# Two of four pairs of attention heads turned by TensorE, twelve weight splits half on GpSimd, and the second matrix's conversions issued behind the Fourier mix

## The chip, the cores and the metric

The kernel runs on one core of a Trainium2 chip. The metric is the device time of one launch, in microseconds; for the kernel before it is 1125.69 us (median of three runs, 1124.08 to 1126.49).

## What is computed

Three blocks follow each other. With four batches of 576 tokens, eight heads of 64, and a model width of 512:

```python
scale = 1.0 / np.sqrt(D)
scores = scale * q @ k.T                       # per batch and head
cum = np.cumsum(np.maximum(s, 0), -1)
bias = -(cum[:, None] - cum[None, :])
scores = np.where(causal, -1e9, scores + np.minimum(bias, 0))
attn = softmax(scores) @ v                     # x: (4, 576, 512)

u = x + np.real(np.fft.fft(np.fft.fft(x, axis=1), axis=2))
y = u + np.maximum(layernorm(u) @ w_ch1, 0) @ w_ch2          # 512 -> 2048 -> 512
out = y + np.maximum((layernorm(y) * g_ln) @ w2_ch1, 0) @ w2_ch2
```

The weight matrices arrive as float64, though the computation is in float32 precision. The kernel takes most products in parts: a number is held as a float16 high half (`hi`) and a float16 rest (`lo`), and three products of halves are summed.

## The kernel before

**Attention.** A batch is worked on in four pairs of heads. A pair's tokens lie in five tiles A0, A1, M, B1, B0, whose causal widths are 129, 257, 320, 448 and 576 keys (`EXT`), that is 2, 3, 3, 4 and 5 key blocks of 128 (`NKB`). A unit is one tile of one head, so a pair has ten units. For a unit, TensorE makes the scores (L1034 and L1039, in fp32 for batches 0 and 1, which are run by `attn_steps32`), VectorE adds the bias and takes the minimum in one reduction (L1040, the name `sc`), and `emit_exp` lets ScalarE take the exponential twice: L777 writes the float16 `hi` into the buffer `p`, L778 writes fp32 in place and accumulates the row sum `rs`. GpSimd clears the columns beyond the width (L776). `emit_lo` subtracts `hi` from the fp32 value to give `lo` (L788, all on GpSimd in batch 0) and then issues DMA transposes on SP's queue, one for each head of B0 and B1 (L792) and one for both heads of each of A0, A1 and M (L800): seven a pair, 14 in two pairs. The transposed halves `pT` are the stationary operand of `emit_pv` (L822, three products a key block), issued five units after the scores, and VectorE normalises the result into `xset` or `xm` (L835).

**Weights of the first MLP.** Class `Weights`: each matrix is cut into 16 pieces of 128x512, pieces 0 to 15 of the first matrix and 16 to 31 of the second, 512 KB each as float64. `load` (L143) fetches a piece on SP's queue into one of nine places of staging (seven tiles of their own and the two halves of `xset_108`). `convert` turns float64 into fp32 by three integer operations on VectorE (L150, L153, L156). `square` (L167) has ScalarE sum the squares. `scale` works out a power of two for a matrix from these sums; the name is `wasc`. `split` makes the halves of a piece: `hi` on ScalarE with the scale (L194), `lo` on VectorE (L195). For pieces named in `POOL1` (none before) or, for the second MLP, `POOLB`, another form is used: ScalarE scales in place (L190) and copies to float16 (L191), and GpSimd subtracts (L192). The generator `prep` runs these as 65 steps: nine loads, 16 conversions of the first matrix, its scale, four splits, six loads, 16 conversions of the second matrix with the other twelve splits between them, and an end. The second matrix is split later, within the MLP.

**What sets the order.** A scheduler orders each engine's instructions by priorities and dependencies; an engine then runs its own list strictly in order. The steps of `prep` are handed out by `more_weights`, which issues them after a score reduction of batch 0's attention: by its end, 42 + `W2PRE` of the 65. The others are given out by `weights_after` in the Fourier mix of batch 0, `QF[n]` after its n-th step. `MARK` = 30 gates batch 1's attention behind the conversion of piece 30.

**Mix and normalisation.** After batch 0's attention, its tokens are folded with a reversed copy (`xo` L1114 on GpSimd, `xe` L1113) and split (`eo`, L1122 and L1123), multiplied along the tokens (`y`, L1141, `yT`, L1145 and L1146) and along the features (`z`, L1182), and added to `x` (`pm` L1197 and L1198, `xset` L1203 to L1205). `emit_ln` takes the statistics (L325 to L363), writes `u` (L348) and turns it by a DMA transpose (`unT`, L349). The first MLP's multiplications begin at L374. They run batch by batch, with the next batch's attention and mix worked in beside them; the second MLP (`wb`) follows.

Of the kernel before, what the change touches and what calls it, by code (L numbers as in the profile page):

```python
# [7 lines left out]
F32 = mybir.dt.float32  # L8
# [3 lines left out]
AF = mybir.ActivationFunctionType  # L12
ALU = mybir.AluOpType
# [6 lines left out]
NPAIR = H // 2  # L20
# [5 lines left out]
A0, A1, M, B1, B0 = range(5)  # L26
EXT = [129, 257, 320, 448, 576]
NKB = [2, 3, 3, 4, 5]
MASKED = -(2.0 ** 120)
KN = {'PVS': (0, 3, 0, 0), 'ORD': ((0, 0, 0), (0, 0, 0), (1, 0, 0), (1, 0, 0)), 'WR4': (1.2, 1.2, 1.2, 1.2), 'W0': 4, 'WRATE': 1.0, 'W2PRE': 18, 'NCONST': 40, 'HOLDN': 1, 'S1': 4, 'S2': 1, 'S1B': 0, 'COST': (1.0, 1.0, 1.0, 1.0, 1.0), 'POOL1': (), 'POOLB': (0, 1, 2, 3, 4, 5, 6, 7), 'QF': (3, 3, 3, 3, 3, 3, 3, 3, 3, 3, 3), 'QL': (1, 1, 1, 1), 'WCALLS': 2, 'WN': 65, 'SPGATE': 0, 'LATE4': 1, 'MARK': 30, 'CJ': (2, 6), 'PVLAG': 7, 'LOLAG': 1, 'PVLAG32': 5, 'PJ32': 4, 'A0OFF': 0, 'A1OFF': 0, 'F0OFF': 300, 'AOFF': (200, 0, 300, 300), 'FOFF': (300, 600, 300, 150), 'LNOFF': (300, 600, 150, 600), 'LOFF': 300, 'PJ': 1, 'PN': 1, 'PL': 6, 'KPREP': 0, 'KPRE': (6, 0, 0), 'KSTEP': ((0, 0, 1), (0, 1), (1,)), 'RATES': (1.9, 1.4, 1.9, 1.2), 'POOLX': (0, 1, 1, 1), 'LO_POOL': ((0, 4, 1, 3, 2), (0, 1, 2, 3), (4,), (0, 1, 2)), 'TAILW': 2, 'LNM': 0, 'LAZY': 8, 'CALLS3': 65, 'N32': 2}  # L30


@with_exitstack
def fused_kernel(ctx: ExitStack, tc, q, k, v, s, wa1, wa2, g_ln, wb1, wb2, tok_c, feat_c, ident_c, rev_c, bias_c, out):
    nc = tc.nc
# [21 lines left out]
    def htile(name, t, h, which):  # L57
        return ring.tile([128, HW[t]], F16, tag=f"h{which}{t}{h}", name=name)

    def htile2(name, t, which):  # L60
        return ring.tile([128, 2 * HW[t]], F16, tag=f"h{which}{t}", name=name)
# [40 lines left out]
    class Weights:  # L102
# [42 lines left out]
        def convert(self, i):  # L145
# [12 lines left out]
            )  # L158
            if i <= KN["MARK"]:
                self.mark = done  # L160
# [52 lines left out]
        def prep(self):  # L213

            for i in range(len(self.wide + self.extra)):
                self.load(i)
                yield KN["COST"][0]
            held = []
            for i in range(16):
# [319 lines left out]
    ident = xpool.tile([128, DM], F32, tag="xm1", name="ident")[:, 0:128]  # L539
# [76 lines left out]
    pairs = {}  # L616
# [127 lines left out]
    def emit_qk(u):  # L744
        P, t, h = pairs[u.p], u.t, u.h
        n = EXT[t]
        cuts = ((0, 288), (288, 576)) if n > 512 else ((0, n),)
        mn = small.tile([128, 2], F32, tag="mn", name="mn", bufs=4)
        kT, qT = P.qkT, q_rows(P, t, h)
        for i, (a, z) in enumerate(cuts):  # L750
            ps = ps_s.tile([128, 512], F32, tag="s", name="s")[:, 0:z - a]
            nc.tensor.matmul(out=ps, lhsT=qT, rhs=kT[:, 2 + h, a:z], start=True, stop=False)
            r = slice(64 * h, 64 * h + 64)
            nc.tensor.matmul(out=ps, lhsT=qT[r], rhs=kT[r, 4, a:z], start=False, stop=True)  # L754
            gate[0] = nc.vector.tensor_tensor_reduce(  # L755
                out=u.f[:, a:z], in0=ps, in1=u.f[:, a:z], scale=P.sc[:, 7:8],
                scalar=mn[:, i - 1:i] if i else 3.0e38, op0=ALU.add, op1=ALU.min, accum_out=mn[:, i:i + 1],
            )
# [95 lines left out]
    N32 = KN["N32"]  # L854

    def attn_steps(b):
# [15 lines left out]
        for i in range(N + KN["PVLAG"]):  # L872
# [23 lines left out]
            if KN["LOLAG"] <= i < N + KN["LOLAG"]:  # L896
                emit_lo(us[i - KN["LOLAG"]])
# [112 lines left out]
    def emit_qk32(u):  # L1010
# [10 lines left out]
        for i, (a, z) in enumerate(cuts):  # L1021
# [16 lines left out]
            if masked:  # L1038
# [283 lines left out]
    if True:  # L1322
# [15 lines left out]
        w = wa.prep()  # L1338
# [152 lines left out]
```

## Time and profile before

| | us |
|---|---|
| runs | 1124.08, 1126.49, 1125.69 |
| median | 1125.69 |
| the profiled execution | 1122.61 |
| its span | 1120.7 |
| TensorE busy | 1005.1 (90%) |
| VectorE busy | 722.8 (64%) |
| ScalarE busy | 569.6 (51%) |
| GpSimd busy | 608.7 (54%) |
| first multiplication of the first MLP (L374) begins | 179.70 |

The profiled execution is one launch seen by the hardware profiler; the span goes from its first to its last instruction. Busy shares are averages over stages with different limits, so the rows further down are taken by stretches of the first 180 us, where the change lies. In the rows PE is TensorE, PEld its weight loads, DVE VectorE, ACT ScalarE, POOL GpSimd and SP the engine that issues most DMAs; L788 is line 788 of the kernel, and `out<-in` are the program's names.

### The profile page before, as it was taken

How to read it: one execution, taken by the hardware profiler on the slowest of the kernel's cores; microseconds unless marked ns; L12 is line 12 of the kernel's file. 1: busy time of each engine (PE TensorE's matmuls, PEld its weight loads, DVE VectorE, ACT ScalarE, POOL GpSimd, SP SyncE). 2: the span in 40 equal slices, each digit the busy share in tenths (PEclk: the TensorE clock that was granted, in tenths of full speed). 3: DMA queues.
4: the chain of work that ended last, by engine and by line, in shares of the span. 5: the costliest groups of instructions: out<-in, count | busy, mean ns of one | idle time of the engine just before them, and what ended most of it. 6: DMA issues, size and time to landing. Idle time of an engine off the chain costs nothing.

```text
span 1120.7 us, 23179 instructions
## 1 busy us (share of the span) xinstructions
PE 1005.1 (90%) x8537; PEld 746.0 (67%) x8537; DVE 722.8 (64%) x1720; ACT 569.6 (51%) x1270; POOL 608.7 (54%) x1298
## 2 busy tenths in 40 slices
PE   5668378988989999889997898998999999999998
PEld 4445245666656566446665675567888888888887
DVE  5978978746798774886746697946544534542333
ACT  5687548764666662566622256643433343443342
POOL 3535658885489640787713106258656546645352
PEclk9878667999999999989999899999999999999999
DMA  7999937666469980289811794102111211211000
GB/s 199 257 201 239 237 106 137 134 132 135 92 123 190 201 183 2 68 163 200 146 36 38 217 310 151 47 1 76 31 46 39 58 20 39 57 39 20 20 8 32
DMA packets 286034, 124.17 MB, mean 111 GB/s; under 512 B 267616, under 2 KB 267872, under 8 KB 285920
## 3 DMA queue, kind: packets, MB, share of 16 engines
q1 hardware_dynamic: 285280, 120.59, 46.6%
q0 software_dynamic: 640, 2.10, 0.6%
q8 instruction: 67, 1.10, 0.4%
q14 instruction: 47, 0.39, 0.1%
HBM read 61.50 MB, written 9.51 MB: 63 GB/s over the span
## 4 chain that ended last, share of the span: by engine, by line
PE 55%; DVE 18%; POOL 7%; DMA 6%; issue 3%; ACT 3%; SPq 1%; POOLq 0%; DVEq 0%; ACTq 0%
PE acc L468 14%; PE g L374 9%; PE g L440 8%; PE g L398 8%; PE g1x L440 8%; DMA pT<-p 3%; PE pv L822 2%; POOL p L788 2%; PE y L1141 1%; PE z L1182 1%; PE s L1034 1%; DVE h L381 1%; PE s L754 1%; POOL sc L732 1%; DVE st L325 1%
## 5 line engine op out<-in xcount | busy, mean ns | idle before, releaser
L374 PE MATMUL g<-unT,wa 128*128 128x256 f16 x1728 | 223.4, 281 | 10.5 <-DMA unT<-u 10.5
L398 PE MATMUL g<-wa,h 128*128 128x512 f16 x864 | 208.1, 383 | 6.6 <-DVE h L381 4.1
L374 PEld LDWEIGHTS <-wa 128*128 128x128 f16 x1728 | 169.4, 101 | 53.7 <-issue 13.2
L454 DVE TENSOR_TENSOR wa<-wa,wa 128x896 f16<-128x896 f32 x72 | 78.9, 1096 | 161.8 <-ACT wa L453 161.7
L468 PE MATMUL acc<-wbbig,wa 128*128 128x256 f16 x1512 | 179.5, 274 | 3.7 <-DVE wa L454 2.4
L440 PEld LDWEIGHTS <-wb 128*128 128x128 f16 x1728 | 169.1, 98 | 20.2
L468 PEld LDWEIGHTS <-wa 128*128 128x128 f16 x1512 | 148.5, 98 | 22.5 <-DVE wa L454 2.8
L398 PEld LDWEIGHTS <-h 128*128 128x128 f16 x864 | 82.4, 99 | 91.4 <-DVE h L381 6.3
L453 ACT CAST wa<-wa 128x896 f16<-128x896 f32 x72 | 67.5, 938 | 142.3 <-POOL wa L451 142.3
L777 ACT ACTIVATE p<-sc,mn 128x576 f16<-128x576 f32 (+4 forms) x160 | 90.5, 578 | 79.3 <-DVE mn L755 26.8
L788 POOL TENSOR_TENSOR p<-sc,p 128x129 f16<-128x129 f32 (+4 forms) x104 | 92.7, 895 | 45.6 <-ACT sc L778 42.2
L450 POOL TENSOR_TENSOR wa<-wa 128x128 f32<-128x128 f32 x72 | 51.8, 720 | 108.1 <-ACT wa L447 108.1
L822 PE MATMUL pv<-v,pT 128*128 128x64 f16 x1632 | 69.9, 199 | 37.1 <-DVE xset L835 12.7
L440 PE MATMUL g1x<-unT,wb 128*128 128x256 f16 x864 | 101.7, 273 | 0.0
L440 PE MATMUL g<-unT,wb 128*128 128x256 f16 x864 | 100.9, 273 | 0.0
L822 PEld LDWEIGHTS <-pT 128*128 128x128 f16 x1632 | 63.3, 102 | 53.3 <-issue 27.2
L778 ACT ACTIVATE sc<-sc,mn 128x576 f32<-128x576 f32 (+4 forms) x160 | 91.9, 575 | 1.8
L732 POOL TENSOR_TENSOR sc<-cumb,ncqs 128x129 f32<-128x129 f32 (+4 forms) x80 | 68.3, 862 | 22.4 <-DVE cumb L642 14.9
L776 POOL MEMSET p<- 128x128 f16 (+1 forms) x160 | 36.7, 249 | 76.0 <-DMA pT<-p 43.7
L1034 PE MATMUL s<-qkT 128*128 128x288 f32 (+4 forms) x192 | 71.4, 468 | 5.5 <-DVE mn L1040 3.0
L381 DVE SCALAR_TENSOR_TENSOR h<-g,h 128x512 f16<-128x512 f32 x72 | 49.1, 682 | 32.6 <-ACT h L380 32.5
L380 ACT ACTIVATE h<-g 128x512 f16<-128x512 f32 x72 | 42.3, 587 | 51.8 <-PE g L374 51.6
(244 smaller groups left out, 1730.7 us busy)
## 6 DMA issues: line engine op xcount, KB each, us to landing
wbbig<-in_moe_w_ch_dram SPq DMA_DIRECT2D x32, 512.0 KB
wa<-in_moe_w_ch_dram SPq DMA_DIRECT2D x21, 512.0 KB
cumb<-cumd SPq DMA_DIRECT2D x24, 288.0 KB
xset<-in_moe_w_ch_dram SPq DMA_DIRECT2D x11, 512.0 KB
x2d<-o SPq DMA_DIRECT2D x18, 256.0 KB
raw<-in_v_dram SPq DMA_DIRECT2D x32, 128.0 KB
out_dram<-wa SPq DMA_DIRECT2D x16, 256.0 KB
raw<-in_k_dram SPq DMA_DIRECT2D x24, 128.0 KB
```

Of the source, the lines that this page charges most:

```text
L374: nc.tensor.matmul(out=ps[:, 256 * i:256 * i + 256], lhsT=ch.w.w1(lw, kk, m + i), rhs=ch.unT[:, 4 * lx + kk, :], start=(n == 0), stop=(n = ...
L398: nc.tensor.matmul(out=ch.ps[j], lhsT=h[:, lh, c:c + 128], rhs=ch.w.w2(lw, m + i), start=(m + i + n == 0), stop=(m + i == MB - 1 and n == 2),)
L440: nc.tensor.matmul(out=ps, lhsT=ch.w.w1(lw, kk, m + 8 * half), rhs=ch.unT[:, 4 * lx + kk, :], start=(n == 0), stop=(n == 11),)
L453: nc.scalar.copy(out=h[:, 0], in_=r[:, 0:7])
L454: nc.vector.tensor_tensor(out=h[:, 1], in0=r[:, 0:7], in1=h[:, 0], op=ALU.subtract)
L468: nc.tensor.matmul(out=acc[key], lhsT=h[:, lh, ia], rhs=b[:, ib, lw], start=(m == 0 and i == 0 and not second), stop=(m == 7 and i == 2 an ...
L732: nc.gpsimd.tensor_tensor(out=u.f[:, 0:n], in0=P.cumb[u.h][:, 0:n], in1=P.ncq[:, t, u.h:u.h + 1].to_broadcast([128, n]), op=ALU.add)
L777: nc.scalar.activation(out=u.w[:, 0:n], in_=u.f[:, 0:n], func=AF.Exp, bias=mn, scale=-1.0)
L778: nc.scalar.activation(out=u.f[:, 0:n], in_=u.f[:, 0:n], func=AF.Exp, bias=mn, scale=-1.0, accum_out=u.rs[:, h:h + 1])
L788: eng.tensor_tensor(out=u.w[:, w:w + n], in0=u.f[:, 0:n], in1=u.w[:, 0:n], op=ALU.subtract)
L822: nc.tensor.matmul(out=ps[:, c], lhsT=pT[:, lp * nb + kb, :], rhs=P.v[:, kb, lv, c], start=(n == 0), stop=(n == 3 * nb - 1),)
L1034: nc.tensor.matmul(out=ps[:, b - a:e - a], lhsT=P.qT[:, o:o + 128], rhs=kt[:, b - k0:e - k0], start=not pe, stop=not pe or (not masked and ...
```

## The change

Three things are changed.

For pairs 0 and 1 of batch 0 (`TURNED` = 2), `emit_exp` takes one exponential only, in fp32 into the buffer `p`, and `emit_lo` hands over to a new function `emit_turn`: TensorE transposes the unit's key blocks in fp32 into a PSUM bank, ScalarE copies the bank to `hi`, and VectorE subtracts `hi` from the bank to give `lo`, both in place of the DMA transpose. A unit of five key blocks does this in two pieces, so two pairs have 24 pieces and 68 transposes.

Twelve pieces of the first matrix (`POOL1`, 4 to 15) are split by the other form, in which GpSimd scales in place (L191 in the new file), ScalarE copies, and GpSimd subtracts (L195 in the new file).

`W2PRE` goes from 18 to 6 and `QF` from three a step to (0, 1, 1, 2, ...). So 48 of the 65 steps are issued in batch 0's attention instead of 60, and 17 instead of 5 in its Fourier mix.

```diff
-KN = {... 'W2PRE': 18, ... 'POOL1': (), ... 'QF': (3, 3, 3, 3, 3, 3, 3, 3, 3, 3, 3), ...}
+KN = {... 'W2PRE': 6, ... 'POOL1': tuple(range(4, 16)), ... 'QF': (0, 1, 1, 2, 2, 2, 2, 2, 2, 2, 1), ...}
...
             if i < 16 and i in (KN["POOL1"] if self.HOLD else KN["POOLB"]):
-                nc.scalar.activation(out=self.raw(i), in_=self.raw(i), func=AF.Copy, scale=sc)
+                if self.HOLD:
+                    nc.gpsimd.tensor_scalar(out=self.raw(i), in0=self.raw(i), scalar1=sc, scalar2=None, op0=ALU.mult)
+                else:
+                    nc.scalar.activation(out=self.raw(i), in_=self.raw(i), func=AF.Copy, scale=sc)
                 nc.scalar.copy(out=dst[:, 0:512], in_=self.raw(i))
                 nc.gpsimd.tensor_tensor(out=dst[:, 512:1024], in0=self.raw(i), in1=dst[:, 0:512], op=ALU.subtract)
...
+        if u.p < TURNED:
...
+            u.w = u.w[:, 0:2 * w].bitcast(F32)
+            if w > n:
+                nc.gpsimd.memset(u.w[:, n:w], 0.0)
+            nc.scalar.activation(
+                out=u.w[:, 0:n], in_=u.f[:, 0:n], func=AF.Exp, bias=mn, scale=-1.0, accum_out=u.rs[:, h:h + 1]
+            )
+            return
...
+    TURNED = NPAIR // 2
+
+    def emit_turn(u):
+
+        P, t, nb = pairs[u.p], u.t, NKB[u.t]
+        w = nb * 128
...
+        for a, z in ((0, nb),) if nb < 5 else ((0, 3), (3, 5)):
+            ps = tp_psum(u.p)[:, 0:128 * (z - a)]
+            for kb in range(a, z):
+                nc.tensor.transpose(
+                    out=ps[:, 128 * (kb - a):128 * (kb - a + 1)], in_=u.w[:, 128 * kb:128 * (kb + 1)], identity=ident
+                )
+            hi = u.pT[:, 128 * a:128 * z]
+            nc.scalar.copy(out=hi, in_=ps)
+            nc.vector.scalar_tensor_tensor(
+                out=u.pT[:, w + 128 * a:w + 128 * z], in0=ps, scalar=1.0, in1=hi, op0=ALU.mult, op1=ALU.subtract
+            )
+        if u.h == 1:
+            nc.gpsimd.tensor_scalar(out=u.rs, in0=u.rs, scalar1=1e-9, scalar2=None, op0=ALU.add)
+
     def emit_lo(u):
+        if u.p < TURNED:
+            emit_turn(u)
+            return
```

Three places show how the instructions move. In the new file's lines, L794 is the former L776, L835 the former L788, L849 the former L802, L1018 the former L971, L1087 the former L1040, L328 the former L325, L1244 and L1245 the former L1197 and L1198, and L1251 and L1252 the former L1204 and L1205. A number behind a name is that of the buffer.

GpSimd, where pair 1 ends and pair 2 begins, after the change (buffers `p_1041` and on are pair 2's):

```order
L1018 MEMSET qkT_105 128x64
L191 TENSOR_SCALAR wa_175<-wa_175,wasc 128x512
L191 TENSOR_SCALAR wa_176<-wa_176,wasc 128x512
L191 TENSOR_SCALAR wa_177<-wa_177,wasc 128x512
L826 TENSOR_SCALAR rs<-rs 128x2
...
L191 TENSOR_SCALAR wa_186<-wa_186,wasc 128x512
L794 MEMSET p_1321 128x2x64
L835 TENSOR_TENSOR p_1041<-sc,p_1041 128x129 x2
L849 TENSOR_SCALAR rs<-rs 128x2
```

All twelve scalings stand ahead of the first `lo` of pair 2; before, nothing of the weights was on this engine here.

VectorE, before the change, from the last two conversions to the first `pm` of the mix:

```order
L150 TENSOR_SCALAR spare<-xset_108 128x512
L1146 SCALAR_TENSOR_TENSOR yT<-y,yT 128x320
L153 SCALAR_TENSOR_TENSOR spare<-xset_108,spare 128x512
L156 SCALAR_TENSOR_TENSOR spare<-xset_108,spare 128x512
L1146 SCALAR_TENSOR_TENSOR yT<-y,yT 128x320
L150 TENSOR_SCALAR spare<-xset_108 128x512
...
L156 SCALAR_TENSOR_TENSOR spare<-xset_108,spare 128x512
L1197 TENSOR_TENSOR pm<-z 128x255
```

And after the change, from behind the first `pm` on:

```order
L1252 TENSOR_TENSOR xset_107<-xset_107,pm 128x255
L150 TENSOR_SCALAR wa_193<-xset_108 128x512
L153 SCALAR_TENSOR_TENSOR wa_192<-xset_108,wa_192 128x512
L328 BN_STATS st<-xset_107 128x6
...
L153 SCALAR_TENSOR_TENSOR wa_193<-xset_108,wa_193 128x512
L156 SCALAR_TENSOR_TENSOR wa_192<-xset_108,wa_192 128x512
L329 BN_AGGR mv<-st 128x2
L1252 TENSOR_TENSOR xm_204<-xm_204,pm 64x255
```

The last five conversions, which stood ahead of the first `pm`, now stand between the additions of the mix and the statistics of the normalisation.

## Rows read from the trace of the kernel before

**Rows 1.** The page: busy us, share and count by engine; TensorE's busy tenths in 40 slices.

```profile
PE 1005.1 (90%) x8537; PEld 746.0 (67%) x8537; DVE 722.8 (64%) x1720; ACT 569.6 (51%) x1270; POOL 608.7 (54%) x1298
...
PE   5668378988989999889997898998999999999998
```

**Rows 2.** Stretches: length, busy us PE, PEld, DVE, ACT, POOL; PEclk, DMA share, GB/s.

```profile
16.50:33.20 16.70, 15.46 (x90) 10.39 (x90) 13.24 (x40) 13.74 (x37) 7.67 (x13) 1.00 0.94 278
33.20:73.30 40.10, 22.47 (x201) 15.64 (x201) 36.50 (x94) 27.03 (x74) 18.61 (x35) 0.74 1.00 216
73.30:93.40 20.10, 18.22 (x150) 12.09 (x150) 13.06 (x50) 17.47 (x45) 9.23 (x21) 0.81 0.98 282
93.40:116.70 23.30, 15.33 (x151) 10.74 (x148) 22.83 (x57) 18.17 (x46) 13.68 (x27) 0.94 0.91 184
116.70:138.20 21.50, 8.47 (x111) 6.80 (x111) 20.60 (x42) 10.30 (x29) 12.57 (x12) 0.53 0.99 245
138.20:156.80 18.60, 14.60 (x90) 8.57 (x90) 11.66 (x25) 7.28 (x20) 10.52 (x20) 0.63 0.48 139
156.80:175.30 18.50, 10.55 (x49) 7.72 (x50) 17.82 (x65) 11.22 (x29) 11.19 (x29) 0.70 0.42 99
...
350.00:560.00 210.00, 198.68 (x1766) 124.91 (x1765) 148.95 (x434) 124.16 (x296) 133.32 (x310) 0.98 0.71 141
```

**Rows 3.** The chain of waits near the prologue's end: start, us, engine or DMA, line.

```profile
168.35 3.94 DMA pT<-p
...
176.45 3.21 DMA unT<-u
179.70 7.78 PE g L374 x48
```

**Rows 4.** Groups by line, whole span, VectorE: busy us, mean ns | idle before, releaser.

```profile
L381 DVE SCALAR_TENSOR_TENSOR h<-g,h 128x512 f16<-128x512 f32 x72 | 49.1, 682 | 32.6 <-ACT h L380 32.5
...
L1146 DVE SCALAR_TENSOR_TENSOR yT<-y,yT 128x320 f16<-128x320 f32 x16 | 7.2, 484 | 15.6 <-ACT yT L1145 15.4
```

**Rows 5.** Groups by line, VectorE, 16.5 to 73.3 us (pairs 0 and 1).

```profile
L156 DVE SCALAR_TENSOR_TENSOR wa<-wa,wa 128x512 int32<-128x512 int32 x14 | 11.2, 801 | 0.0
L153 DVE SCALAR_TENSOR_TENSOR wa<-wa,wa 128x512 int32<-128x512 int32 x14 | 11.2, 811 | 0.0
L150 DVE TENSOR_SCALAR wa<-wa 128x512 int32<-128x512 int32 x14 | 9.2, 660 | 0.0
```

**Rows 6.** Two of these lines by themselves: shortest, median and longest in ns.

```profile
L150 DVE TENSOR_SCALAR wa<-wa x14: 410/426/1502, 24.7 to 67.1; 128x512 int32<-128x512 int32 x14
...
L153 DVE SCALAR_TENSOR_TENSOR wa<-wa,wa x14: 668/678/1765, 26.5 to 67.6; 128x512 int32<-128x512 int32 x14
```

**Rows 7.** Groups by line, GpSimd, 16.5 to 73.3 us.

```profile
L788 POOL TENSOR_TENSOR p<-sc,p 128x129 f16<-128x129 f32 (+4 forms) x19 | 18.4, 970 | 20.7 <-ACT sc L778 20.6
```

**Rows 8.** Groups by line and form, whole span: TensorE's fp32 transposes of 128x128.

```profile
L974 PE MATMUL tp<-ident,qk 128*128 128x128 f32 x16 | 2.9, 313 | 0.0
```

**Rows 9.** Groups by line, 73.3 to 116.7 us (pairs 2 and 3): the splits.

```profile
L194 ACT ACTIVATE wa<-wa,wasc 128x512 f16<-128x512 f32 x13 | 9.2, 714 | 1.7 <-DVE wasc L97 1.1 <-DVE wa L195 0.4
L195 DVE SCALAR_TENSOR_TENSOR wa<-wa,wasc,wa 128x512 f16<-128x512 f32 x11 | 8.8, 802 | 0.0
```

**Rows 10.** Groups by line and form, whole span, GpSimd: one input, two inputs.

```profile
L737 POOL TENSOR_SCALAR_AFFINE_SELECT sc<-sc 128x128 f32<-128x128 f32 x96 | 34.4, 365 | 2.2
...
L192 POOL TENSOR_TENSOR wb<-wb,wb 128x512 f16<-128x512 f32 x8 | 11.0, 1401 | 7.3 <-ACT wb L191 7.3
```

**Rows 11.** Timeline, 116 to 140 us: start, us, engine, line, operation.

```profile
116.67 0.48 DVE L1040 CUSTOM_DVE_ANT_0 sc<-s,zero 128x320 f32<-128x320 f32 x1
...
119.24 4.38 POOL L788 TENSOR_TENSOR p<-sc,p 128x320 f16<-128x320 f32 x2
...
132.31 0.34 SPq L143 DMA_DIRECT2D xset<-in_moe_w_ch_dram  x1
...
137.22 0.41 DVE L150 TENSOR_SCALAR wa<-xset 128x512 int32<-128x512 int32 x1
```

More of the change, by code (lines that the diff above doesn't have):

```diff
@@ L29 @@
 MASKED = -(2.0 ** 120)
-KN = {'PVS': (0, 3, 0, 0), 'ORD': ((0, 0, 0), (0, 0, 0), (1, 0, 0), (1, 0, 0)), 'WR4': (1.2, 1.2, 1.2, 1.2), 'W0': 4, 'WRATE': 1.0, 'W2PRE': 18, 'NCONST': 40, 'HOLDN': 1, 'S1': 4, 'S2': 1, 'S1B': 0, 'COST': (1.0, 1.0, 1.0, 1.0, 1.0), 'POOL1': (), 'POOLB': (0, 1, 2, 3, 4, 5, 6, 7), 'QF': (3, 3, 3, 3, 3, 3, 3, 3, 3, 3, 3), 'QL': (1, 1, 1, 1), 'WCALLS': 2, 'WN': 65, 'SPGATE': 0, 'LATE4': 1, 'MARK': 30, 'CJ': (2, 6), 'PVLAG': 7, 'LOLAG': 1, 'PVLAG32': 5, 'PJ32': 4, 'A0OFF': 0, 'A1OFF': 0, 'F0OFF': 300, 'AOFF': (200, 0, 300, 300), 'FOFF': (300, 600, 300, 150), 'LNOFF': (300, 600, 150, 600), 'LOFF': 300, 'PJ': 1, 'PN': 1, 'PL': 6, 'KPREP': 0, 'KPRE': (6, 0, 0), 'KSTEP': ((0, 0, 1), (0, 1), (1,)), 'RATES': (1.9, 1.4, 1.9, 1.2), 'POOLX': (0, 1, 1, 1), 'LO_POOL': ((0, 4, 1, 3, 2), (0, 1, 2, 3), (4,), (0, 1, 2)), 'TAILW': 2, 'LNM': 0, 'LAZY': 8, 'CALLS3': 65, 'N32': 2}
+KN = {'PVS': (0, 3, 0, 0), 'ORD': ((0, 0, 0), (0, 0, 0), (1, 0, 0), (1, 0, 0)), 'WR4': (1.2, 1.2, 1.2, 1.2), 'W0': 4, 'WRATE': 1.0, 'W2PRE': 6, 'NCONST': 40, 'HOLDN': 1, 'S1': 4, 'S2': 1, 'S1B': 0, 'COST': (1.0, 1.0, 1.0, 1.0, 1.0), 'POOL1': tuple(range(4, 16)), 'POOLB': (0, 1, 2, 3, 4, 5, 6, 7), 'QF': (0, 1, 1, 2, 2, 2, 2, 2, 2, 2, 1), 'QL': (1, 1, 1, 1), 'WCALLS': 2, 'WN': 65, 'SPGATE': 0, 'LATE4': 1, 'MARK': 30, 'CJ': (2, 6), 'PVLAG': 7, 'LOLAG': 1, 'PVLAG32': 5, 'PJ32': 4, 'A0OFF': 0, 'A1OFF': 0, 'F0OFF': 300, 'AOFF': (200, 0, 300, 300), 'FOFF': (300, 600, 300, 150), 'LNOFF': (300, 600, 150, 600), 'LOFF': 300, 'PJ': 1, 'PN': 1, 'PL': 6, 'KPREP': 0, 'KPRE': (6, 0, 0), 'KSTEP': ((0, 0, 1), (0, 1), (1,)), 'RATES': (1.9, 1.4, 1.9, 1.2), 'POOLX': (0, 1, 1, 1), 'LO_POOL': ((0, 4, 1, 3, 2), (0, 1, 2, 3), (4,), (0, 1, 2)), 'TAILW': 2, 'LNM': 0, 'LAZY': 8, 'CALLS3': 65, 'N32': 2}
 @with_exitstack
@@ L767, in emit_exp @@
         w = NKB[t] * 128
+        if u.p < TURNED:
+            if t in (B0, B1):
+                u.w = htile("p16", t, h, 0)
+            else:
+                if h == 0:
+                    P.w[t] = htile2("p16", t, 0)
+                u.w = P.w[t][:, 2 * w * h:2 * w * (h + 1)]
+            u.w = u.w[:, 0:2 * w].bitcast(F32)
[5 more added lines that the diff above has]
+            return
         if t in (B0, B1):
@@ L782, in fused_kernel @@
     gate = [None, None, None, None]
+    TURNED = NPAIR // 2
+    def emit_turn(u):
+        P, t, nb = pairs[u.p], u.t, NKB[u.t]
+        w = nb * 128
+        if t in (B0, B1):
+            u.pT = htile("pT", t, u.h, 1)
+        else:
+            if u.h == 0:
+                P.pT[t] = htile2("pT", t, 1)
+            u.pT = P.pT[t][:, 2 * w * u.h:2 * w * (u.h + 1)]
+        for a, z in ((0, nb),) if nb < 5 else ((0, 3), (3, 5)):
[11 more added lines that the diff above has]
+            nc.gpsimd.tensor_scalar(out=u.rs, in0=u.rs, scalar1=1e-9, scalar2=None, op0=ALU.add)
     def emit_lo(u):
+        if u.p < TURNED:
+            emit_turn(u)
+            return
         t = u.t
```

## The prediction

> **What bounds the kernel now.** I read the page first, then a table of busy time by stretch, then the chain of waits. Over the whole span TensorE is busy 90% and VectorE 64% [rows 1], which reads as a TensorE kernel, and from the first multiplication of the first MLP on (179.70 us) it is one: in the stretch from 350 to 560 us TensorE works 198.68 of 210 us [rows 2]. The slices of its row begin with 5, 6, 6, 8, though [rows 1]: what comes before is bound by something else. The stretches [rows 2] are batch 0's four pairs of heads (the last score reduction of each ends at 33.2, 73.3, 93.4 and 116.7), the tail of that attention until the last normalise, the mix until the first `pm`, and the rest of the mix with the normalisation until `u`. VectorE is busy 13.24 of 16.7, 36.50 of 40.1, 22.83 of 23.3 (pair 3), 20.60 of 21.5 (tail) and 17.82 of 18.5 (rest of the mix and LN). Only pair 2 (TensorE 18.22 of 20.1, at a granted clock of 0.81) and the first part of the mix (VectorE 11.66 of 18.6) have another limit. The chain [rows 3] ends the prologue with the turning of `u` and then runs on in TensorE. So a shift of 179.70 should reach the end nearly whole, and the change must be priced as **VectorE time before that moment**, stretch by stretch.
>
> **Pairs 0 and 1 (16.5 to 73.3).** Removed: one of two exponentials per unit, the subtraction for `lo` on GpSimd, and all 14 DMA transposes of these pairs with SP's waits for them. Added: 68 fp32 transposes on TensorE (17 key blocks per pair and head), and 24 pieces turned, each with a ScalarE copy and a VectorE subtraction out of PSUM. The trace has two subtractions of the same form [rows 4]: 484 ns for 320 columns and 682 for 512, about 1.03 ns a column. So 256 columns take 0.42, 384 take 0.55, 512 take 0.68; eight, twelve and four of these are 3.3 + 6.6 + 2.7 = **12.7 us** more for VectorE. It is idle 7.1 of the 56.8 us, in gaps; I let a quarter of that, 1.7, take up some of it, and 11 stay. Against it stands relief. The conversions average 660, 811 and 801 ns here [rows 5] while their shortest are 410 and 668 (L156 has L153's form, and I use its value) [rows 6]: 14 x (0.25 + 0.143 + 0.133) = 7.4 us is lost to something. The other engine at work on SBUF is GpSimd, whose 18.4 us of `lo` [rows 7] vanish here. Bounds: relief of 0 to 7.4. I take all of it, since memsets and tiny operations are what GpSimd keeps. The balance is **+3.5**.
> The Trainium skill ("SBUF — State Buffer", Who interferes with whom) says that a VectorE operation with two SBUF inputs contends with a GpSimd operation that reads SBUF, and one with at most one SBUF input does not. By that the PSUM-fed turn pays nothing and L153 and L156 get relief; the spread between the shortest and the mean agrees, though no run here yet separates the causes.
> TensorE's transposes: 16 like ones are 2.9 us busy [rows 8], 0.18 each, so 12.3 us; by the mean of one, 313 ns, 21.3. TensorE idles 18.9 us in this stretch, which covers the first. ScalarE exchanges an exponential for a copy: nothing. If that cover went, the turns themselves would be on the path (rival 2).
>
> **Pairs 2 and 3 (73.3 to 116.7).** Twelve splits leave VectorE at 802 ns each (eleven of them stand in this stretch, 8.8 us, six in pair 3), while ScalarE keeps its part, 714 ns each [rows 9], as a copy. Pair 3, full on VectorE, loses 4.8 us and gains one conversion (six instead of five), 1.75 below, which leaves -3.1; with conversions a little less disturbed I take -4 (the floor is ScalarE's 18.2, -5.1). Pair 2 is TensorE's, 18.2 of 20.1, and its splits free nothing but gaps: -1.5. Against that GpSimd gets twelve scalings at once and twelve subtractions. A subtraction has its row, 1401 ns; a scaling has none: the nearest are 365 ns for one input of 128 columns and the 1401 for two inputs of 512 [rows 10]. I take 0.7, half of the latter, because it reads half as much; the ends are 0.37 and 1.40, so twelve are 8.4, with ends 4.4 and 16.8. They wait for the scale, which is ready some 2 us before pair 1's last reduction, and in GpSimd's order all stand ahead of pair 2's first `lo`. That is about 6 us of delay for a `lo` that before came 3 us after the pair's start; the probabilities are used only five units later, so it is nearly covered. GpSimd then has 22.9 + 8.4 + six subtractions 8.4 = 39.7 us, 2 of it ahead of the pair, against 37.9 left: just full. I take **-5.5**.
>
> **The tail (116.7 to 138.2).** Its 20.6 us of VectorE are mostly seven conversions and five splits, none of which stand there any more. What is left is a chain: reduction at 116.67, `lo` started 2.57 later [rows 11], two `lo` at their mean of 0.97 [rows 7] instead of 4.38, the transposition 3.94 [rows 3], its multiplications and the normalise, 2 to 3 us. That is 11.2 in place of 21.5: **-10.3**.
>
> **Mix, and normalisation.** The pieces that left come back here. Each conversion is at least 0.41 + 0.67 + 0.67 = 1.75 us. One more than before (five for four) falls before the first `pm`, where VectorE has 6.9 us idle: I take half, **+0.9** (ends 0 and 1.75). Five fall between `pm` and the second `u` (pieces 27 to 31, where before has none): 8.7 us into 0.7 us of idle time: **+8.0**. These stand between the statistics of the normalisation, in VectorE's own order, so each delays `u`, its DMA transposition and the first multiplication.
>
> **Sum.** +3.5 - 5.5 - 10.3 + 0.9 + 8.0 = -3.4 us. The profiled execution took 1122.61 (span 1120.7, and 1.9 around it), 3.1 below the median of the three runs, 1125.69. The shift is applied to the median: **1122.3 us**. A difference of 0.2%, 2.3 us, is about what a measurement of this kernel can tell from none.
>
> **Rivals.**
> 1. More is gained. If pair 2 is slow because of the transposes' SP queue and a lowered clock, and pairs 0 and 1 hide the turns in VectorE's gaps, the first term becomes 0 and the second -9: -10.4, **1115.3**. For: VectorE's idle 7.1 us; GpSimd's `lo` gone. Against: VectorE's gaps there are short waits for TensorE, which gets more to do.
> 2. The turns cost full price (slower). TensorE, ScalarE and VectorE must follow each other for every piece with few banks between, and each VectorE subtraction stands in order ahead of the next conversion or reduction. With no relief and no gap used, the first term is 12.7 and the sum +5.8: **1131.5**. It decides from +9.2 on in pairs 0 and 1. For: VectorE busy 36.50 of 40.1.
> 3. The late loads stall the normalisation (slower). Pieces 27 to 31 share two places of staging, so a load is issued only when the one before is converted; 4.9 us from issue (132.31) to conversion (137.22) [rows 11]. Two such waits exposed in VectorE's order add 9.8: +6.4, **1132.1**.
> 4. GpSimd is the bound of pairs 2 and 3. At 1.40 a scaling, 8.4 us more: +5.0, **1130.7**. It decides where a scaling takes over 1.2, from which the sum is above +2.3.
> The Trainium skill ("Perfetto Trace Analysis", Optimizing Scalar/DVE Operations) warns that moving work from VectorE to GpSimd might not help since they share a port. By it the twelve scalings and subtractions would lengthen VectorE's conversions as `lo` did, and give rival 4 or the next.
> 5. A wash. VectorE's work is only exchanged: +12.7 for turns, -9.6 for twelve splits, conversions the same in number: +3.1, less half of the relief, 3.7: -0.6, **1125.1**. For: every stretch but two is VectorE's.
>
> **How the numbers follow.** Forecast (-2.3 to -7) 0.27; rival 1 0.20; rival 5 (within 2.3) 0.20; rival 2 0.13; rival 3 0.11; rival 4 0.09. Faster by over 0.2%: 0.27 + 0.20 = 0.47; within: 0.20; slower: 0.33. The range takes in rival 1 with the tail shorter by a further 4 us, and rivals 2 to 4 with some 2 us over: 1111 to 1134. The likeliest case alone is 1118.7 to 1123.4.
>
> **What would show it.** Right: the last reduction of pair 1 near 77, of pair 3 near 114, the last normalise near 126, the second `u` near 171 and the first multiplication near 176; conversions in pairs 0 and 1 near 0.45 and 0.7 us. Wrong: pair 1 ending past 82 (rival 2); VectorE idle in front of L150 with a DMA as releaser between `pm` and `u` (rival 3); `lo` in pair 2 begun over 10 us after its exponential, or TensorE waiting for `pT` there (rival 4); or a first multiplication earlier by more than the end is, which would say that the rest is not TensorE's alone.

## The result, and the profile after

The changed kernel takes 1133.54 us (median of seven runs, 1129.80 to 1135.75) against 1125.24 in the same job: a ratio of 1.0068, 95% interval 1.0052 to 1.0085, so 7.7 us **slower** where 3.4 us faster was forecast (the ratio goes by all the runs; the two medians are 8.3 us apart). The profiled execution took 1133.93 us, span 1132.2, 11.5 more than that of before; 2.6 of this is that before's traced execution lay below its median.

The same stretches as in [rows 2], cut at the same events (columns as there; each event is taken at its start; the tail and the mix are divided at the last normalise, 132.7, and the last row ends where VectorE's second `u` starts, 174.6 before, while the row of before runs to that `u`'s end):

```profile
15.90:34.60 18.70, 18.08 (x148) 13.73 (x147) 15.71 (x52) 13.50 (x40) 2.60 (x13) 1.00 0.86 262
34.60:74.00 39.40, 28.39 (x260) 20.81 (x261) 36.66 (x104) 26.63 (x78) 4.07 (x16) 0.83 0.84 258
74.00:89.30 15.30, 13.48 (x88) 9.09 (x88) 11.82 (x48) 15.23 (x40) 14.04 (x10) 0.89 0.22 61
89.30:114.30 25.00, 15.02 (x120) 9.65 (x120) 22.33 (x50) 14.45 (x42) 24.05 (x31) 0.86 0.68 144
114.30:132.70 18.40, 9.14 (x144) 7.84 (x143) 5.21 (x17) 7.37 (x19) 17.82 (x31) 0.51 1.05 210
132.70:154.50 21.80, 17.68 (x99) 9.75 (x99) 20.17 (x32) 10.01 (x24) 17.61 (x29) 0.56 0.14 50
154.50:181.80 27.30, 9.72 (x41) 7.24 (x38) 25.03 (x76) 14.41 (x40) 20.02 (x46) 0.62 0.50 136
```

| stretch (end before, end after) | forecast | traces |
|---|---|---|
| pairs 0 and 1 (73.3, 74.0) | +3.5 | +0.7 |
| pairs 2 and 3 (116.7, 114.3) | -5.5 | -3.1 |
| tail, to the last normalise (138.2, 132.7) | -10.3 | -3.1 |
| mix, to the first `pm` (156.8, 154.5) | +0.9 | +3.2 |
| to the second `u` (174.6, 181.8) | +8.0 | +9.5 |
| all that follows (1120.7, 1132.2) | 0 | +4.3 |
| sum | -3.4 | +11.5 |

Pair 3 and the tail have a new bound: GpSimd, the fifth busy time of a row, works 24.05 of 25.0 and 17.82 of 18.4 us, where VectorE had 22.83 of 23.3 and 20.60 of 21.5 before [rows 2]. Its own timeline at the start of pair 2 (start, us, engine, line, operation):

```profile
75.08 5.18 POOL L191 TENSOR_SCALAR wa<-wa,wasc 128x512 f32<-128x512 f32 x3 [1.08 <-DVE wasc L97]
...
80.66 15.12 POOL L191 TENSOR_SCALAR wa<-wa,wasc 128x512 f32<-128x512 f32 x9
...
95.90 0.82 POOL L835 TENSOR_TENSOR p<-sc,p 128x129 f16<-128x129 f32 x2
...
97.17 2.95 POOL L835 TENSOR_TENSOR p<-sc,p 128x576 f16<-128x576 f32 x2
```

The scalings fill 75.1 to 95.8, and the first `lo` of pair 2 starts at 95.9, though the scores of that unit were reduced at 74.4 and the pair's last reduction starts at 89.3. The two lines by themselves (shortest, median, longest in ns; first and last start):

```profile
L191 POOL TENSOR_SCALAR wa<-wa,wasc x12: 1558/1570/2242, 75.1 to 94.2; 128x512 f32<-128x512 f32 x12
```

```profile
L195 POOL TENSOR_TENSOR wa<-wa,wa x12: 1147/1214/1663, 105.7 to 146.9; 128x512 f16<-128x512 f32 x12
```

A scaling costs 1.57 us in the median and 1.71 in the mean (twelve are 20.3 us busy), above the 0.7 that I took and above the upper end of 1.40 as well. The last subtractions start at 147; only two of the twelve stand in pairs 2 and 3, ten in the tail and the mix. The chain of waits (start, us, engine or DMA, line) shows it from 85 to 132; what is left out between 97 and 127 is nearly all GpSimd's too:

```profile
85.29 10.49 POOL wa L191 x6
...
97.17 2.95 POOL p L835 x2
...
126.31 1.11 POOL wa L195
127.50 0.22 POOL rs L849
127.76 3.73 DMA pT<-p
131.53 1.15 PE pv L869 x18
...
165.10 3.33 DMA xset<-in_moe_w_ch_dram
168.45 0.43 DVE wa L150
```

Its last rows are the second place: a conversion within the normalisation stands behind the load of its piece. The load takes 3.3 us, but VectorE has other work meanwhile; in this whole stretch it idles 0.8 us in front of a conversion for a load.

### The profile page after: what moved, and what is told of

It is laid out like the page before. It is cut to its first block, busy times and chain, and to the rows that moved or that the text cites. A ratio compares the mean times of both kernels' runs of the same rounds, so it can differ in the third digit from the quotient of the medians.

```text
span 1132.2 us, 23307 instructions
## 1 busy us (share of the span) xinstructions
PE 1015.4 (90%) x8605; PEld 753.3 (67%) x8605; DVE 724.0 (64%) x1732; ACT 567.2 (50%) x1274; POOL 617.3 (55%) x1302
## 4 chain that ended last, share of the span: by engine, by line
PE 54%; DVE 18%; POOL 10%; DMA 7%; ACT 6%; issue 4%; SPq 1%; POOLq 0%; ACTq 0%; DVEq 0%
PE acc L471 14%; PE g L443 8%; PE g1x L443 8%; PE g L377 7%; PE g L401 7%; POOL p L835 3%; DMA pT<-p 2%; PE pv L869 2%; PE s L1081 2%; PE y L1188 2%; DVE h L384 1%; PE z L1229 1%; POOL sc L735 1%; DMA unT<-u 1%; DVE sc L758 1%
## 5 line engine op out<-in xcount | busy, mean ns | idle before, releaser
L401 PE MATMUL g<-wa,h 128*128 128x512 f16 x864 | 212.4, 388 | 7.7 <-DVE h L384 4.5
L443 PEld LDWEIGHTS <-wb 128*128 128x128 f16 x1728 | 169.1, 98 | 20.3
L795 ACT ACTIVATE p<-sc,mn 128x448 f16<-128x448 f32 (+4 forms) x140 | 78.6, 577 | 61.4 <-DVE mn L758 26.7
L869 PE MATMUL pv<-v,pT 128*128 128x64 f16 x1632 | 71.6, 200 | 20.6 <-DMA pT<-p 14.8
L1081 PE MATMUL s<-qkT 128*128 128x288 f32 (+4 forms) x192 | 68.4, 453 | 19.6 <-DVE total L84 14.2
L796 ACT ACTIVATE sc<-sc,mn 128x448 f32<-128x448 f32 (+4 forms) x140 | 80.4, 575 | 1.4
L835 POOL TENSOR_TENSOR p<-sc,p 128x129 f16<-128x129 f32 (+4 forms) x84 | 70.2, 840 | 9.5 <-ACT sc L796 8.8
L794 POOL MEMSET p<- 128x128 f16 (+1 forms) x140 | 32.4, 247 | 77.0 <-DMA pT<-p 35.0
## 6 DMA issues: line engine op xcount, KB each, us to landing
raw<-in_v_dram SPq DMA_DIRECT2D x32, 128.0 KB
raw<-in_k_dram SPq DMA_DIRECT2D x24, 128.0 KB
```

The costliest lines, as they stand in the source:

```text
L401: nc.tensor.matmul(out=ch.ps[j], lhsT=h[:, lh, c:c + 128], rhs=ch.w.w2(lw, m + i), start=(m + i + n == 0), stop=(m + i == MB - 1 and n == 2),)
L443: nc.tensor.matmul(out=ps, lhsT=ch.w.w1(lw, kk, m + 8 * half), rhs=ch.unT[:, 4 * lx + kk, :], start=(n == 0), stop=(n == 11),)
L796: nc.scalar.activation(out=u.f[:, 0:n], in_=u.f[:, 0:n], func=AF.Exp, bias=mn, scale=-1.0, accum_out=u.rs[:, h:h + 1])
L869: nc.tensor.matmul(out=ps[:, c], lhsT=pT[:, lp * nb + kb, :], rhs=P.v[:, kb, lv, c], start=(n == 0), stop=(n == 3 * nb - 1),)
L1081: nc.tensor.matmul(out=ps[:, b - a:e - a], lhsT=P.qT[:, o:o + 128], rhs=kt[:, b - k0:e - k0], start=not pe, stop=not pe or (not masked and ...
```

## The experiments

Each part was run alone and in every combination, then the causes by themselves. Differences below are the ratio to the kernel before, times 1126 us.

**1. The turned pairs alone.**

```diff
-'W2PRE': 6, 'POOL1': tuple(range(4, 16)), 'QF': (0, 1, 1, 2, 2, 2, 2, 2, 2, 2, 1)
+'W2PRE': 18, 'POOL1': (), 'QF': (3, 3, 3, 3, 3, 3, 3, 3, 3, 3, 3)
```

> Two pairs turned by TensorE, all else as before. Theory A (GpSimd's twelve scalings at 1.57 us and twelve subtractions bound the attention of pairs 2 and 3 and its tail): no GpSimd splits here, so at or below the 1125.2 of before, 1119 to 1126, with pair 1 ending near 74. Theory B (the conversions within the normalisation cost it): the same, 1119 to 1126. Theory C (the turns cost it): 1130 or more.

1129.64 (12 runs), ratio 1.0018 [1.0002, 1.0035]: +2.0. Not above 1130, and no gain either: A and B forecast at most 1126. The twelve runs spread over 7.6 us, the 21 of before beside them over 5.1; runs 8 and 13 come back to that.

**2. The changed kernel without GpSimd's splits** (`POOL1` empty).

> The changed kernel with no piece split on GpSimd: the turned pairs and the late conversions stay. A: GpSimd is free when pair 2 begins, the score reduction of pair 3 ends at 113 to 116 and the last normalise at 126 to 130; 1121 to 1127. B: still 1131 or more. C: 1131 or more, with the loss already there before 74 us.

1131.28 (10 runs, 1125.24 to 1137.50), 1.0053 [1.0034, 1.0072]: +6.0, only 1.7 less than the whole change. In the trace the tail and the mix are short, 14.5 and 15.8 us, and pair 3's last reduction and the last normalise are at 113.5 and 128.0, as A says (run 8 has the rows of a second trace of this kernel), yet the time stays where B and C put it. So A alone isn't the account.

**3. Scalings on ScalarE.**

```diff
-                if self.HOLD:
+                if False:
                     nc.gpsimd.tensor_scalar(out=self.raw(i), in0=self.raw(i), scalar1=sc, ...)
```

> The changed kernel with the twelve scalings on ScalarE (0.6 us each, 7 us) in place of GpSimd (1.57 us each, 19 us); the subtractions stay on GpSimd. A: GpSimd begins the first lo of pair 2 within 5 us of its exponentials, and the time is 1121 to 1128. If the subtractions alone (12 of 1.2 us) are enough to bind: 1130 to 1134. B: 1131 to 1135.

1137.82, 1.0097 [1.0078, 1.0115]: +10.9, worse than every guess. The same work now holds ScalarE: the twelve scalings take 7.7 us there, six of them in one row between two exponentials of pair 2, in which it works 24.09 of 24.5 us (17.47 of 20.1 before).

```profile
75.30:99.80 24.50, 15.58 (x107) 10.63 (x106) 15.06 (x52) 24.09 (x55) 9.60 (x16) 0.79 0.27 63
```

GpSimd is no freer behind it: the subtractions and `lo` alone keep it at 20.02 of 20.7 us in pair 3 and 18.39 of 18.9 in the tail. So this run says that ScalarE has no room for the scalings either; it doesn't separate their order from their amount.

**4. Early conversions**, with the turned pairs and GpSimd's splits (`W2PRE` and `QF` as before).

> The changed kernel with the 65 steps handed out as before (60 in the attention, 5 in the mix); turned pairs and GpSimd splits stay. A: GpSimd still starts pair 2's lo some 15 us late, so it stays slow, 1129 to 1135. B: the normalisation has no conversion in it, 1121 to 1127.

1144.37, 1.0161 [1.0145, 1.0176]: +18.1. B is out: with no late conversion the loss is larger. Most of it stands in the mix, 30.6 us against 18.6. The conversions now meet GpSimd's subtractions. Between 100 and 160 us, L156 from the `xset` places:

```profile
L156 DVE SCALAR_TENSOR_TENSOR wa<-xset,wa x7: 904/1257/1634, 112.5 to 151.1; 128x512 int32<-128x512 int32 x7
```

With the turned pairs alone, and GpSimd free of splits, the same line in the same stretch:

```profile
L156 DVE SCALAR_TENSOR_TENSOR wa<-xset,wa x7: 674/678/1519, 115.8 to 146.2; 128x512 int32<-128x512 int32 x7
```

In all, VectorE's 48 conversion instructions between 74 and 190 us (L150, L153, L156) take 49.2 us here and 35.3 in run 1. The 13.9 us are more than twelve splits take from VectorE: at run 1's mean of 930 ns they are 11.2.

**5. GpSimd's splits alone** (no pair turned, early conversions).

> The kernel before with the twelve GpSimd splits alone: no pair turned, conversions as before. A (twelve scalings in one row hold GpSimd, and with it the lo of the pair that follows): 8 to 18 us slower than before, the loss between 73 and 157 us, larger in the mix than in pair 2. D (the splits cost only together with the turned pairs): within 3 us of before.

1143.85, 1.0142 [1.0113, 1.0171]: +16.0, A. Pair 2 takes 40.8 us instead of 20.1, and GpSimd's timeline says why:

```profile
73.70:114.50 40.80, 19.30 (x178) 14.03 (x178) 15.34 (x54) 19.90 (x51) 34.73 (x42) 0.67 0.82 223
```

```profile
73.69 7.74 POOL L191 TENSOR_SCALAR wa<-wa,wasc 128x512 f32<-128x512 f32 x5
...
81.56 10.80 POOL L191 TENSOR_SCALAR wa<-wa,wasc 128x512 f32<-128x512 f32 x7
92.32 0.79 POOL L835 TENSOR_TENSOR p<-sc,p 128x320 f16<-128x320 f32 x1
```

A `lo` of the pair before waits until 92.3. The place was expected in the mix above all; it is pair 2.

**6. Late conversions alone** (no pair turned, no GpSimd split).

> The kernel before with the late conversions alone: 17 steps in the mix, no pair turned, no GpSimd split. B (conversions within the normalisation cost more than the tail gains): 2 to 8 us slower, with the tail of the attention shorter by 5 to 8 us and the stretch from the first pm to the second u longer by 9 to 14. Rival (the tail gains as much): within 2 us of before.

1124.41 (12 runs), 0.9979 [0.9965, 0.9993]: -2.4. A miss of B, and nearer the rival: the tail shrinks by 8 (21.5 to 13.5), the normalisation grows by 10.5 (17.8 to 28.3), and the kernel is a little faster. Tail, mix and normalisation:

```profile
112.90:126.40 13.50, 8.21 (x111) 6.26 (x111) 8.69 (x20) 4.93 (x16) 8.79 (x15) 0.62 0.96 240
126.40:146.80 20.40, 15.17 (x94) 9.15 (x94) 18.30 (x37) 11.67 (x26) 11.53 (x20) 0.67 0.66 168
146.80:175.10 28.30, 9.04 (x37) 6.28 (x37) 25.74 (x78) 13.81 (x37) 20.01 (x42) 0.66 0.45 124
```

**7. Six of the twelve pieces scaled only behind the last `xo`.**

```diff
-            with tc.issue_after(ins.ins):
+            with tc.issue_after(ins.ins), tc.issue_after(gate[4].ins):
```

(`gate[4]` is GpSimd's last `lo` or `xo`; the edit holds every step handed out in the mix behind it, the late conversions too.)

> The changed kernel, in which pieces 10 to 15 are scaled and subtracted on GpSimd only behind the last xo of the mix; pieces 4 to 9 as changed. Same work on every engine. A: six scalings of 1.57 us fewer stand ahead of pair 2's first lo, so it begins 9 us earlier; attention ends 4 to 9 us earlier, and the time is 2 to 8 us below the changed kernel's, 1126 to 1132. B: the loss is in the normalisation, so within 2 us of the changed kernel.

1136.65, 1.0071 [1.0050, 1.0093]: +8.0, the changed kernel's time. A forecast 2 to 8 less. From pair 1's end to the second `u` the trace has 104.3 us against 107.8: pair 3 fell from 25.0 to 20.1 and the mix from 21.8 to 18.0, while the tail and the normalisation took 20.4 and 29.5. But pair 1, which the edit doesn't touch, ends at 77.7 instead of 74.0, and what follows the second `u` takes 954.0 instead of 950.4. So moving half of the burst gains little; whether its order or its amount costs more isn't settled by this run.

**8. Run 2 again, for a second trace.**

> The kernel without GpSimd splits once more, for a second trace: its times lay between 1125.2 and 1137.5, and the traced one was the lowest. If the spread comes from the conversions that wait for their loads between pm and u, this stretch differs from the 31.4 us of the first trace by most of the difference in time; if it comes from the first MLP, first multiplication and time part company by as much.

1132.09, and 5.2 of the 6.9 us against the first trace arise in pair 1, whose last reduction is at 78.1 instead of 72.9; pair 0 ends alike. Neither expected place. In the first trace, between 55 and 65 us, TensorE had its full clock:

```profile
55.00:65.00 10.00, 5.93 (x50) 4.45 (x48) 10.00 (x25) 8.13 (x24) 1.37 (x4) 1.00 0.76 232
```

In the second, a granted 0.61, a mean nearer the lower of its two levels (1.2 GHz of 2.4), with fewer matmuls, and the stretches from pair 2's end on as short as in the first:

```profile
55.00:65.00 10.00, 5.77 (x21) 3.53 (x22) 10.00 (x26) 5.54 (x17) 0.20 (x1) 0.61 0.83 263
```

```profile
119.50:134.00 14.50, 7.31 (x99) 5.76 (x98) 8.92 (x18) 4.76 (x16) 12.25 (x21) 0.56 0.91 179
134.00:149.80 15.80, 12.65 (x81) 7.72 (x82) 14.89 (x33) 9.05 (x20) 2.72 (x6) 0.68 0.18 58
149.80:180.90 31.10, 10.81 (x57) 8.53 (x56) 26.42 (x79) 15.35 (x41) 25.30 (x50) 0.66 0.47 131
```

These three are the tail, the mix and the normalisation of run 2's kernel. Tail and mix are 9.9 us shorter than in the changed kernel; 3.8 of it goes in the normalisation.

**9. One pair turned, late conversions** (`TURNED` = 1, `POOL1` empty).

> Late conversions, no GpSimd split, and only pair 0 turned by TensorE. So far: late conversions alone -2.4 us against before, with two pairs turned +6.0. Theory E (pair 1's turns put TensorE into the chain at that pair's end, where its last scores stand behind turns and the multiplications by v, and its granted clock decides): with pair 1 on the DMA transposes again the last reduction of pair 1 is at 72 to 74 us and the time within 2 us of late alone, 1122 to 1127. Rival F (each turned pair costs the same): halfway, 1127 to 1131.

1134.19, 1.0062 [1.0044, 1.0079]: +7.0, as much as with two pairs. Both theories fail: neither pair 1's turns nor an equal price for each pair accounts for it. The waits of TensorE between 52 and 75 us (what waited for what: us in all, times, longest) gave the next idea. One pair turned:

```profile
PE total L82 <- ACT v L1039: 6.4, 1, 6.4
```

All three parts, the changed kernel:

```profile
PE total L82 <- ACT v L1039: 3.1, 1, 3.1
```

Late alone:

```profile
PE total L82 <- ACT v L1039: 1.5, 1, 1.5
```

And the kernel before, where L992 is the later L1039:

```profile
PE total L82 <- ACT v L992: 2.5, 1, 2.5
```

That is the total over pair 2's `v`, from which its scale is worked out, and TensorE reaches it in its order before pair 1's last scores. SP's queue had held the loads of the mix's tables back behind its DMA transposes; without these it sends them before pair 2's `v`. SP's timeline, before and then changed:

```profile
86.30 0.43 SPq L1341 DMA_DIRECT2D tok<-in_tok_dram  x1
```

```profile
37.06 0.50 SPq L1388 DMA_DIRECT2D tok<-in_tok_dram  x1
```

The waits alone don't bear this out: `v` itself is sent at 51.3 before and at 52.4 in the changed kernel (61.7 with one pair turned), and the wait of before is nearly as long as the changed kernel's. What speaks for it is run 8's chain of waits (start, us, engine or DMA, line), which passes through `v`:

```profile
55.64 3.94 DMA raw<-in_v_dram
60.56 0.59 PE total L82 x2
```

So do the chains of runs 3, 4 and 7, and in these four traces pair 1 ends at 75.3 to 78.1. Those of the changed kernel and of run 2's first trace don't, at 74.0 and 72.9.

**10. Late conversions and GpSimd's splits, no pair turned.**

> Late conversions and twelve GpSimd splits, no pair turned; with this all eight combinations of the three parts are measured. A: the scalings stand ahead of pair 1's last lo and all of pair 2's, as in the run of the GpSimd splits alone, where pair 2 took 40.8 us; 8 to 18 us slower than before. D (late conversions make the GpSimd splits nearly free, as they do beside the turned pairs, +1.7): 1125 to 1129.

1143.67, 1.0157 [1.0134, 1.0180]: +17.7, A; D is out. GpSimd's splits cost 16.0 alone, 16.1 beside the turned pairs, 20.1 beside late conversions, and 1.7 beside both.

**11. Before again, for a second trace.**

> The kernel before once more, for a second trace: the first was 3 to 4 us below its median. If the spread of single runs comes from pair 1 as it does with two pairs turned (72.9 and 78.1 us at its last reduction), pair 1 ends later than 73.3 by most of the difference; otherwise the difference lies behind the first multiplication at 179.7.

1126.90. Pair 1 ends at 71.7, not later; the first multiplication of the MLP is at 181.4 instead of 179.7, and what follows takes 943.7 instead of 941.0 us. So traces of one kernel differ by 2.7 us behind the first multiplication. Counted from the second `u`, as in the table's last row, they differ by 3.9 us, and the +4.3 there is hardly more.

**12. Half of the conversions late, nothing else.**

```diff
-'W2PRE': 18, 'QF': (3, 3, 3, 3, 3, 3, 3, 3, 3, 3, 3)
+'W2PRE': 12, 'QF': (0, 1, 1, 1, 1, 1, 1, 1, 1, 1, 2)
```

> A version that might beat both: no pair turned, no GpSimd split, and half of the conversions moved (54 steps in the attention, 11 in the mix). If the gain of the tail (8.1 us with 17 steps in the mix) and the loss behind the first pm (10.5) both go by the number moved, it lies between before and late alone, -1.2 +- 2; if the loss comes only from the last two loads, which are waited for, it is 2 to 5 below late alone.

1122.57 (10 runs), 0.9964 [0.9952, 0.9976]: -4.1, **the version that beats both kernels**. Tail, mix and normalisation:

```profile
116.60:133.70 17.10, 8.62 (x111) 7.00 (x111) 15.40 (x30) 7.75 (x22) 10.56 (x12) 0.51 1.07 244
133.70:149.60 15.90, 13.60 (x90) 8.38 (x90) 13.82 (x28) 7.86 (x20) 8.95 (x19) 0.68 0.63 168
149.60:173.00 23.40, 11.63 (x53) 8.24 (x50) 22.57 (x73) 13.69 (x36) 18.38 (x32) 0.59 0.44 118
```

Against [rows 2] the tail gives 4.4 and the mix 2.7, the normalisation takes 5.6: more gain and less loss than moving all 17 steps. The second `u` is 1.6 us earlier; the first multiplication, at 180.6, is no earlier than the 179.7 and 181.4 of before, so where the rest of the 4.1 arises isn't shown. The point estimate is 1.7 below late alone, just short of what the second clause asked; the intervals overlap, so that half is better than all isn't shown.

**13. Run 2's kernel with the tables' loads later.**

```diff
-            if n == KN["NCONST"]:
-                consts()
+            if gate[1] is not None and not late_consts:
+                with tc.issue_after(gate[1].ins):
+                    consts()
+                late_consts.append(n)
```

> Two pairs turned, late conversions, no GpSimd split, and the loads of tok, feat and rev queued behind pair 2's first DMA transpose, as they were before the pairs were turned. Theory G (with the transposes gone SP sends the tables ahead of pair 2's q, k and v, so v comes late and TensorE waits in order): TensorE's wait for the total of v falls from 3 to under 1.5 us, pair 1 ends at 70 to 74, and the time is 3 to 8 us below the run with the tables early, 1123 to 1128. Theory H (the turns on TensorE themselves, behind which pair 1's last scores stand): within 2 us of it, 1129 to 1133.

1124.72 (12 runs, 1120.49 to 1134.10), 0.9985 [0.9962, 1.0008]: -1.7, so 7.7 us below run 2. By its time, G: the two intervals together leave some 4 to 11 us for the order of the loads beside late conversions. `tok` is sent at 82.2, `v` already at 48.5, and the wait for its total is gone from the list. How the time is gained is less clear. This trace (1127.47, above its median) has pair 1's end at 74.0, later than run 2's first. Over all traces with two pairs turned it lies between 72.9 and 78.1 with the tables early (seven, mean 75.6) and between 71.6 and 74.0 with the tables later (three, mean 73.1). So about 2.5 us are seen there, and the rest isn't located.

**14. Half late, two pairs turned, tables later.**

> Half of the conversions late (-4.1 us against before without turned pairs), two pairs turned, tables later, no GpSimd split. G: 1119 to 1125, as good as half-late alone or better. H: 4 to 9 us above half-late alone, 1126 to 1132.

1129.26, 1.0019 [1.0005, 1.0033]: +2.1, 6.2 above half late alone, as H has it. But the loss isn't where H puts it: the first multiplication of the MLP starts at 175.8, earlier than in half late alone, 180.6. It is given back behind it: the rest takes 951.6 us instead of 939.6. The first quarter of the first MLP's first-matrix multiplications, here and then in half late alone:

```profile
175.80:347.60 171.80, 158.05 (x1375) 106.70 (x1375) 126.75 (x359) 115.21 (x275) 128.67 (x274) 0.97 0.70 133
```

```profile
180.60:345.90 165.30, 156.11 (x1353) 106.57 (x1353) 123.75 (x353) 112.19 (x266) 124.51 (x269) 0.96 0.66 133
```

TensorE has 22 more matmuls in it and idles 4.6 us more. Part of the early start is thus work that has moved behind it; what work, why the idle time grows, and where the rest of the 12.0 goes, stays open. So here two turned pairs cost 6.2 us even with the tables later.

**15. The changed kernel with the tables' loads later.**

> The changed kernel, all three parts, with the loads of tok, feat and rev queued behind pair 2's first DMA transpose. If the order of the loads is the larger part (it was worth 7.7 us without GpSimd's splits), 1125 to 1129. If GpSimd's scalings are, since pair 2 then waits for them instead of for v, within 3 us of the changed kernel: 1131 to 1136, with the tail and the mix together still at 38 us or more.

1135.29, 1.0085 [1.0070, 1.0099]: +9.6, no better than the change itself: pair 1 ends at 71.6 instead of 74.0, and pair 3 at 114.1 instead of 114.3. GpSimd takes up what the loads give. (The tail and the mix together are 37.3, just under the 38 expected.) Where it has no splits (run 13) the time is 11.3 us lower; that is what GpSimd's splits cost in this kernel with the tables later. With the tables early it was 1.7 (run 2). That the loads' order hides the rest there is the likeliest reading, but the traces don't show it: this one, 1129.87, is the fastest of its six runs and only 2.4 us above run 13's.

## Why the prediction was wrong

**The step that failed is GpSimd's account in pairs 2 and 3**, and after it the tail and the mix. I took 0.7 us for a scaling between 0.37 and 1.40 from [rows 10], wrote "just full" for the attention, and let no work of GpSimd reach the tail, though six of the twelve subtractions were left over for it. A scaling measured 1.57 in the median. Twelve were 20.3 us instead of 8.4, all ahead of pair 2's `lo`, and six subtractions at 1.2 follow in between until 131; GpSimd is full from 75 to then. The scale, too, was ready 1.0 us after pair 1's last reduction and not some 2 before it; before the change it was ready 0.5 before it. My -10.3 and +0.9 for tail and mix came out as -3.1 and +3.2, 9.5 of the 14.9 us between forecast and traces. Without GpSimd's splits, in run 2's kernel, the two stretches are 14.5 and 15.8 us, 30.3 together where the forecast's terms make 30.7. Rival 4 was this mechanism, with its sign (a `lo` over 10 us after its exponential; here it was 18), priced from the same wrong end at 1130.7 and given 0.09; the order listing showed the twelve in one row, and that alone should have brought more. The time is still within the stated range only because that was stretched for rivals 2 to 4; the direction was wrong.

**A missing term: the loads that move up on SP's queue.** I counted the 14 DMA transposes as removed work and did not ask what had stood behind them. The tables' loads moved from 86 to 37 us. Run 13 prices their order at 7.7 us beside late conversions; that it acts through a late `v` is seen in four traces, not in the changed kernel's own, where `v` was sent only 1.1 us later than before. In the changed kernel undoing either cause changes nothing clear of noise (run 2: -1.7; run 15: +1.9), and undoing both gives 9.4 us. The two overlap; how, stays open.

**Right: the relief of VectorE.** Here the conversions of pairs 0 and 1:

```profile
L150 DVE TENSOR_SCALAR wa<-wa x14: 409/414/429, 24.9 to 63.0; 128x512 int32<-128x512 int32 x14
```

```profile
L153 DVE SCALAR_TENSOR_TENSOR wa<-wa,wa x14: 660/674/683, 27.0 to 66.5; 128x512 int32<-128x512 int32 x14
```

Means of 660 and 811 [rows 5] have fallen to 414 and 674, and L153's longest is 683 where it was 1765 [rows 6]. GpSimd's `lo` is gone from here, and so are the DMA transposes; that it was `lo` fits run 4, where GpSimd's subtractions lengthen L156, but these pairs alone don't separate the two. The Trainium skill ("SBUF — State Buffer", Who interferes with whom) says this of a VectorE operation with two SBUF inputs, such as L153, and the run agrees; L150 reads one input and was disturbed too, which that sentence doesn't cover. For one input the section excepts VectorE's 2-port modes, which the prediction left out; no run shows whether L150 is in one. A turn's subtraction took 521 ns in the mean, 0.53 forecast. The term +3.5 came out as +0.7, with -0.4 to +4.8 over the seven traces with two pairs turned and the tables early: their mean is +2.3, so of the good +0.7 a part is luck.

**Right in sign: the normalisation**, +9.5 for +8.0. Of the 1.5 more, VectorE's idle time for loads in front of conversions can be 0.8, under a tenth of rival 3's price of 9.8; the rest isn't traced.

**The passing through.** A later `u` was passed on: 7.1 us at the second `u`, 7.7 in the ratio. An earlier first multiplication was not in run 14. The first multiplication is a mark of the prologue only if the same work stands ahead of it.

**What the splits gave VectorE.** The Trainium skill warns that moving work between VectorE and GpSimd might not help ("Perfetto Trace Analysis", Optimizing Scalar/DVE Operations). Run 4 agrees: L156 at 1257 ns instead of 678, and 13.9 us more for all conversions than in run 1. In the changed kernel the conversions between 74 and 190 us take 38.6 us against 32.6 in run 2. My term for pair 3 had them "a little less disturbed". How much of the loss is this, and how much GpSimd's own queue, no run separates.

## What to carry to other kernels

Before work goes to an engine with spare time, look at where its instructions land in that engine's order: a burst that becomes ready at once stands in front of the stage's own work and can hold it back by its whole length, whatever the busy share says (pair 2's first `lo` began 18 us after its exponential). Price the burst by a row of the same operation; where there is none, measure it. And ask what the work does to the engine that it leaves: in run 4 VectorE lost as much as it was spared. When waits leave a DMA queue, list what moves up in it and whose load now comes later. Two causes that hide each other need the run with both undone; undone singly, neither gave more than 1.7 of 9.4 us.

## What the runs showed of the hardware that was not expected

- On GpSimd, scaling 128x512 fp32 by a value per partition took 1558 ns at the least, longer than subtracting two tiles of that size (1147), though it reads one and not two.
- One kernel's traces differed by 5.2 us in pair 1, with a granted clock of TensorE of 1.00 in one and 0.61 in the other between 55 and 65 us; in the slower one TensorE waited 2.9 us for the total of `v` (1.5 in the other). Which of the two brings the other isn't shown.
